# Four pairs of heads a cycle instead of two an iteration, scores and values side by side, in a fused attention and MLP kernel

## The chip, the cores and the metric

The kernel runs on one core of one Trainium2 chip. The metric is device time in microseconds; lower is better. One profiled execution stands beside the timed runs.

## What is computed

Three stages follow each other on a batch of 2, 768 positions, 8 heads of 64, so a model width of 512. All arrays are float32.

```python
# 1. attention: keys 0..7 (global) and the last 96 (local), with a slope per head
scores = scale * q @ k.T + bias          # masked elsewhere with -1e9
a = exp(scores - max); a = a / (sum(a) + 1e-9)
x = a @ v                                 # heads side by side: (2, 768, 512)
# 2. MLP with a layer norm in front
xn = (x - mu) / sqrt(var + 1e-6) * g_ln
x = x + max(xn @ w_ch1, 0) @ w_ch2        # 512 -> 2048 -> 512
# 3. mixing
theta = x @ w_theta
y = w_tok_r @ (x * cos(theta)) + w_tok_i @ (x * sin(theta))
u = x + y
out = u + max(u @ w_ch, 0)
```

## The kernel before, in words

The 1536 positions are cut into twelve blocks of 128 queries. Heads go in pairs (four pairs `p` to a block), so that a pair fills 128 partitions: a score matmul uses 64 rows of TensorE's array for each head, two heads side by side; a value matmul uses 64 columns for each.

A block passes through these steps. `scores` (L224) multiplies queries with up to 256 window keys into two PSUM banks, one for each head of a pair. `soften` (L206) adds the bias and takes the row maximum on VectorE (L213), then the exponential on ScalarE (L220), into a tile `e`. `flip_probs` (L246) transposes `e` on TensorE into a bank `pt` and copies it out, even pairs on ScalarE (L256), odd pairs on VectorE (L258), to `pts`. `values` (L261) multiplies with the values into the bank `xa`. `lift_x` (L279) copies `xa` out on ScalarE; `finish_x` (L284) transposes it back (`xp`, L292) and multiplies with the reciprocal row sums into `x2`. `layer_norm` (L300) makes `xn` on VectorE; `make_xt` (L386) transposes it (`xnp`, L321) and splits it into a high and a low part, `xth` on ScalarE and `xtl` on VectorE.

The MLP then runs on chunks of two blocks. Each product is three matmuls in TensorE's faster float32 form (high x high, high x low, low x high). `mlp_h` (L399) is the up projection of one slice `f` of 128 hidden units: twelve matmuls into a bank `hp`, then relu and the split `hh`, `hl`. `mlp_o` (L430) is the down projection: three matmuls for each of the chunk's two blocks into the banks `op`; with the last slice of a group the result is added to `x2` on VectorE (L428).

The weights lie in memory as 64-bit words. SyncE loads a piece of 128 x 512 (`raw`), and `decode` (L343) puts its float32 value together again: ScalarE makes one part, and for the first 16 pieces VectorE makes the rest in three operations (L359 to L361), for all later ones ScalarE makes the low bits too (L355) and VectorE needs two (L356, L357). `split_w` (L370) makes the high part on ScalarE and the low part on GpSimd (first four slices) or VectorE.

The first two blocks are a startup of eight steps (`head_step`, L823), with matmuls of zeros (`spin`, L75) in its gaps. They have only 128 keys. Then comes the stage that the change rewrites: ten blocks of attention together with the first four hidden slices of all six chunks, 24 items `(c, f)`. TensorE's order is written out by hand there (`manual_schedule`, L874); the other engines' order comes from the framework's scheduler, in which the program's order is the priority, and `behind_exp`, `behind_maximum` and `tc.issue_after` hold an instruction behind another one on its own engine. One iteration `k` of the loop (L875) has a unit of two pairs, `unit(k)`, and the item `j = k - 3`:

1. transposes of the first pair of unit `k - 1`, scores of unit `k`;
2. half of the up projection, transposes of the second pair, the other half;
3. in every second iteration `make_xt`, in the others `finish_x` within the down projection of item `j - 1`;
4. the values of unit `k - 1`, and after a block's second unit `lift_x`;
5. at a low priority a decoded and split piece (`k` up to 5) or a decoded one for the next group.

The PSUM banks have tags: `h` (2) for `hp` and `xnp`, `o` (2) for `op`, `s` (2) for scores, `pt` (1) for transposed probabilities and `xp`, `m` (1) for `xa`. Behind this stage follow the other hidden slices, with chunks of four blocks, and the mixing.

Of the kernel before, what the change touches and what calls it, by code (L numbers as in the profile page):

```python
# [8 lines left out]
F32 = mybir.dt.float32  # L9
# [4 lines left out]
AF = mybir.ActivationFunctionType  # L14
# [14 lines left out]
GROUP = 4  # L29
EDGE = 248  # L30
NE = 4
NPT = 2

PAD = 24

# [2 lines left out]
def kernel(ctx, tc, q, kwin, v, n_pair, g_ln, wall, out):  # L38
# [33 lines left out]
    def ps(tag, shape, name):  # L72
        return bank(tag, shape, name, BANKS[tag])

    def spin(tag, name, n):  # L75

        o = ps(tag, [P, DM], name)
        for _ in range(n):
            nc.tensor.matmul(o, zero[:, 0:P], zero, start=True, stop=True)  # L79
# [46 lines left out]
    def behind_maximum(n):  # L126
        return tc.issue_after(maxima[n]) if n is not None else ExitStack()
# [96 lines left out]
    def scores(b, i, ps_, startup):  # L224

        nk = WIN if i else P
        if ps_[0] == 0:
            stat[b, i] = (
                at.tile([P, H], F32, tag="nm", name=f"nm{b}_{i}", bufs=2),
                at.tile([P, H], F32, tag="sm", name=f"sm{b}_{i}", bufs=2),  # L230
            )
        qb, kb = qt[b, i], kt[b, i]
        n = len(ps_)
        s = [ps("h" if startup and ps_[0] % 2 else "s", [P, n, nk], f"s{b}_{i}_{ps_[0]}_{j}") for j in range(2)]
        k0 = WIN - nk
        for a, p in enumerate(ps_):
            for j in range(2):
                rows = slice(j * D, (j + 1) * D)
                nc.tensor.matmul(s[j][:, a, :], qb[rows, p, :], kb[rows, p, k0:WIN], start=True, stop=True)  # L239
        if startup:  # L240
            spin("o", f"spin{b}_{ps_[0]}", 2)
        for a, p in enumerate(ps_):
            e = at.tile([P, 2, nk], F32, tag="p", name=f"e{b}_{i}_{p}", bufs=NE)
            soften(b, i, p, e, [s[j][:, a, :] for j in range(2)])

    def flip_probs(b, i, p, startup):  # L246
        nb = 2 if i else 1
        e = e_t.pop((b, i, p))
        pt_tag = "o" if startup and p % 2 else "pt"
        pt = ps(pt_tag, [P, 2, nb, P], f"pt{b}_{i}_{p}")  # L250
        for j in range(2):
            for c in range(nb):
                nc.tensor.transpose(pt[:, j, c, :], e[:, j, c * P:(c + 1) * P], ident)  # L253
        pts = at.tile([P, 2, nb, P], F32, tag="pt", name=f"pts{b}_{i}_{p}", bufs=NPT)
        if p % 2 == 0:
            nc.scalar.activation(pts, pt, AF.Copy)  # L256
        else:
            nc.vector.tensor_copy(pts, pt)  # L258
        pts_t[b, i, p] = pts
# [18 lines left out]

    def lift_x(b, i):  # L279
        xs = at.tile([P, NPAIR, P], F32, tag="xs", name=f"xs{b}_{i}", bufs=1)  # L280
        nc.scalar.activation(xs, xa_t.pop((b, i)), AF.Copy)
        xs_t[b, i] = xs

    def finish_x(b, i, startup):  # L284
        t = b * NQ + i
        nm, sm = stat.pop((b, i))
        xs = xs_t.pop((b, i))
        nc.vector.tensor_scalar(sm, sm, 1.0e-9, None, ALU.add)
        nc.vector.reciprocal(sm, sm)
        xp = ps("o" if startup else "pt", [P, H, D], f"xp{t}")  # L290
        for p in range(NPAIR):
            nc.tensor.transpose(xp.rearrange("q h d -> q (h d)")[:, p * P:(p + 1) * P], xs[:, p, :], ident)  # L292
        nc.vector.tensor_tensor(  # L293
            x2[t].rearrange("q (h d) -> q h d", d=D), xp, sm.unsqueeze(2).to_broadcast([P, H, D]), ALU.mult
        )
# [47 lines left out]
    def decode(i, out):  # L343

        n = n_decoded[0]
        n_decoded[0] += 1
        load_to(n)
        assert order[n] == i
        r = stage.pop(i)
        load_to(n + NRAW)  # L350
        nc.scalar.activation(out, r.bitcast(F32)[:, :, 1], AF.Copy, scale=2.0**-112)
        t = rawp.tile([P, DM], I32, tag="dec", name=f"dec{i}", bufs=1)
        o = out.bitcast(I32)
        if i >= 4 * GROUP:
            nc.scalar.activation(t, r.bitcast(U32)[:, :, 0], AF.Copy, scale=2.0**-29 * (1 - 2.0**-15), bias=-0.4999)  # L355
            nc.vector.scalar_tensor_tensor(t, o, 3, t, ALU.logical_shift_left, ALU.bitwise_or)  # L356
            nc.vector.scalar_tensor_tensor(o, r[:, :, 1], -2**31, t, ALU.bitwise_and, ALU.bitwise_or)  # L357
            return
        nc.vector.tensor_scalar(t, o, 3, None, ALU.logical_shift_left)  # L359
        nc.vector.scalar_tensor_tensor(t, o, -2**31, t, ALU.bitwise_and, ALU.bitwise_or)  # L360
        nc.vector.scalar_tensor_tensor(o, r[:, :, 0], 29, t, ALU.logical_shift_right, ALU.bitwise_or)  # L361
# [439 lines left out]
    def loads_to(n):  # L801
        while nloaded[0] <= min(n, len(blocks) - 1):
            b, i = blocks[nloaded[0]]
            load_qk(b, i)
            load_v(b, i)
            nloaded[0] += 1
# [38 lines left out]
        head_step(n)  # L845
    for n in range(4, HEAD * NPAIR):
        head_step(n)
        for d, m in enumerate((11, 13)):
            if n == m // 2:
                with behind_exp(m):  # L850
                    split_w(0, (d,))
        if n == 7:
            layer_norm(SEQ[0])
    with behind_maximum(7):
        test_n()

    U = 2
    NU = (NTT - HEAD) * U
    LEAD = 3
    items = [(c, f) for c in range(NCH) for f in GROUPS[0]]  # L860

    def unit(k):
        t, h_ = divmod(k, U)
        return (*blocks[HEAD + t], [2 * h_, 2 * h_ + 1])

    def down(j, js):
        c, f = items[j]
        mlp_o(c, f, GROUPS[0], js)
        if js[-1] and c == NCH - 1 and f + GROUP < NF:
            split_w(f + GROUP)  # L870

    HN = HEAD * NPAIR
    ENGINES = {getattr(mybir.EngineType, e) for e in ("PE",)}
    with tc.manual_schedule(engines=ENGINES):  # L874
        for k in range(LEAD + len(items) + 1):  # L875
            j = k - LEAD
            u = k - 1
            mix = 0 <= j < len(items)
            xp_of = HEAD + (k - 3) // U if k % U == 1 and 0 <= (k - 3) // U < NTT - HEAD else None
            xt_of = HEAD + (k - 4) // U if k % U == 0 and 0 <= (k - 4) // U < NTT - HEAD else None  # L880
            if k == 0:
                flip_probs(*blocks[1], 2, True)
                values(*blocks[1], 1)
                flip_probs(*blocks[1], 3, True)
                spin("o", "idle0", 5)
            if k == 1:
                values(*blocks[1], 2)
                values(*blocks[1], 3)
                lift_x(*blocks[1])
            if 0 <= u < NU:  # L890
                flip_probs(*unit(u)[:2], unit(u)[2][0], False)
            if k < NU:
                b, i, ps_ = unit(k)
                if k % U == 0:
                    loads_to(HEAD + k // U + 2)
                scores(b, i, ps_, False)
            if k == 1:
                make_xt(SEQ[0])
                finish_x(*blocks[1], True)
                layer_norm(SEQ[1])  # L900
            if k == 2:
                make_xt(SEQ[1])
            if mix:
                mlp_h(*items[j], "h", 0)
            elif 0 < k < LEAD:
                spin("o", f"idle{k}", 5)
            if 0 <= u < NU:
                flip_probs(*unit(u)[:2], unit(u)[2][1], False)
            if mix:
                mlp_h(*items[j], "h", 1)  # L910
            if xt_of is not None:
                make_xt(SEQ[xt_of])
            if 0 <= j - 1 < len(items):
                down(j - 1, [0])
            if xp_of is not None:
                finish_x(*blocks[xp_of], False)
            if 0 <= j - 1 < len(items):
                down(j - 1, [1])
            if 0 < k < LEAD:
                spin("o", f"wait{k}", 5)  # L920
            if 0 <= u < NU:
                for p in unit(u)[2]:
                    values(*unit(u)[:2], p)
                if u % U == U - 1:
                    lift_x(*unit(u)[:2])
            if xp_of is not None:
                layer_norm(SEQ[xp_of])
            if 0 <= k < 2 * GROUP - 2:
                with behind_exp(len(maxima) - 1):
                    split_w((k + 2) // 2, ((k + 2) % 2,))  # L930
            elif k >= 7:
                with behind_maximum(min(len(maxima) - 1, 16 + 4 * k + 3)):
                    decode_to(2 * GROUP + min(NW, (k - 5) // 2))

    work = [(g, c, f) for g in range(1, len(GROUPS)) for c in range(len(WIDE)) for f in GROUPS[g]]
    SPAN = len(WIDE) * GROUP
# [116 lines left out]
```

## Time and profile before

| what | value |
|---|---|
| median of 3 runs | 552.93 us (552.78 to 553.32) |
| profiled execution | 553.05 us, its span 551.3 us |
| TensorE busy | 538.8 us (98%), granted clock 0.998 |
| TensorE weight loads busy | 441.1 us (80%) |
| VectorE busy | 367.1 us (67%) |
| ScalarE busy | 275.9 us (50%) |
| GpSimd busy | 18.8 us (3%) |

The profiled execution's time is measured around the whole program, its span from the first to the last instruction in the trace. Busy times are a sum over the span, in which the stages have different limits. Matmuls overlap: an instruction's duration in the trace is longer than the step from one start to the next, and the step is what a matmul costs.

### The profile page before, as it was taken

The numbers are of one execution on the slowest core, as the hardware profiler recorded it, in microseconds if no ns is written. First come the engines' busy times: TensorE is split into PE (matmuls) and PEld (weight loads), VectorE is DVE, ScalarE is ACT, GpSimd is POOL, SyncE is SP. The second block draws the span as 40 slices with busy tenths as digits, with TensorE's granted clock in tenths as the row PEclk, the third lists the DMA queues.
The fourth block names the chain that finished last, engine by engine and source line by source line (L and its number), as shares of the span: only waits on it lengthen the run. The fifth ranks groups of instructions, "written<-read, shape, count | busy, mean of one in ns | idle before, by whom it ended". The sixth has DMA issues, their size and how long they took to land.

```text
span 551.3 us, 8231 instructions
## 1 busy us (share of the span) xinstructions
PE 538.8 (98%) x3122; PEld 441.1 (80%) x3125; DVE 367.1 (67%) x807; ACT 275.9 (50%) x611; POOL 18.8 (3%) x31
## 2 busy tenths in 40 slices
PE   9699999999999999999999999999999999999996
PEld 4367888878878888888888888788888888888896
DVE  5888787878766454544548867895897679921542
ACT  4677765555524232323245646964795566820110
POOL 1222200000000000000000000000000000000000
PEclk9999999999999999999999999999999999999999
DMA  8945544421120123202233263231310000000112
GB/s 272 331 147 195 183 137 155 154 95 39 40 77 1 39 80 111 76 1 76 82 110 115 77 217 125 78 115 39 110 44 0 1 0 2 1 0 15 63 72 87
DMA packets 18543, 49.10 MB, mean 89 GB/s; under 512 B 2241, under 2 KB 4289, under 8 KB 18497
## 3 DMA queue, kind: packets, MB, share of 16 engines
q1 hardware_dynamic: 18496, 48.51, 26.2%
q8 instruction: 26, 0.43, 0.3%
q14 instruction: 21, 0.16, 0.1%
HBM read 45.35 MB, written 3.15 MB: 88 GB/s over the span
## 4 chain that ended last, share of the span: by engine, by line
PE 92%; DVE 3%; ACT 3%; issue 1%
PE hp L415 24%; PE op L440 24%; PE acc L615 18%; PE thm L538 6%; PE ch L661 6%; PE s L239 4%; PE pt L253 3%; PE xa L272 3%; ACT e L220 2%; PE spin L79 1%; PE xnp L321 1%; PE xp L321 1%; PE xp L292 1%; DVE xn L312 1%; DVE x2all L293 0%
## 5 line engine op out<-in xcount | busy, mean ns | idle before, releaser
L615 PE MATMUL acc<-tokh,z 128*128 128x256 f32 (+1 forms) x384 | 95.4, 336 | 0.0
L415 PE MATMUL hp<-xth,w1h 128*128 128x512 f32 (+1 forms) x240 | 86.6, 361 | 0.0
L415 PE MATMUL hp<-xtl,w1h 128*128 128x512 f32 (+1 forms) x240 | 83.2, 347 | 0.0
L415 PE MATMUL hp<-xth,w1l 128*128 128x512 f32 (+1 forms) x240 | 83.0, 346 | 0.0
L440 PE MATMUL op<-w2h,hh 128*128 128x512 f32 x192 | 76.9, 400 | 0.0
L420 ACT ACTIVATE hh<-hp 128x512 fp32r<-128x512 f32 (+1 forms) x60 | 30.3, 505 | 89.9 <-PE hp L415 89.7
L440 PE MATMUL op<-w2h,hl 128*128 128x512 f32 x192 | 75.1, 391 | 0.0
L440 PE MATMUL op<-w2l,hh 128*128 128x512 f32 x192 | 74.9, 390 | 0.0
L420 DVE SCALAR_TENSOR_TENSOR hl<-hp,hh 128x512 fp32r<-128x512 f32 (+1 forms) x60 | 34.8, 581 | 59.4 <-ACT hh L420 59.2
L615 PEld LDWEIGHTS acc<-tokh,z 128*128 128x128 f32 x384 | 66.6, 190 | 8.0
L615 PE MATMUL acc<-tokl,z 128*128 128x512 f32 (+1 forms) x192 | 64.5, 336 | 0.0
L220 ACT ACTIVATE e<-e,nm 128x256 f32<-128x256 f32 (+1 forms) x96 | 46.0, 481 | 22.1 <-DVE nm L213 22.0
L415 PEld LDWEIGHTS hp<-xth,w1h 128*128 128x128 f32 x240 | 45.2, 188 | 11.6 <-issue 3.8
L415 PEld LDWEIGHTS hp<-xtl,w1h 128*128 128x128 f32 x240 | 45.2, 188 | 5.9 <-DVE xtl L323 0.2
L415 PEld LDWEIGHTS hp<-xth,w1l 128*128 128x128 f32 x240 | 45.2, 188 | 5.7
L213 DVE CUSTOM_DVE_ANT_0 e<-s,bias 128x256 f32<-128x256 f32 (+1 forms) x96 | 33.4, 397 | 17.0 <-PE s L239 16.8
L440 PEld LDWEIGHTS op<-w2h,hl 128*128 128x128 f32 x192 | 36.1, 188 | 8.0 <-DVE hl L420 0.2
L440 PEld LDWEIGHTS op<-w2l,hh 128*128 128x128 f32 x192 | 36.2, 189 | 6.2
L440 PEld LDWEIGHTS op<-w2h,hh 128*128 128x128 f32 x192 | 36.1, 188 | 6.2
L615 PEld LDWEIGHTS acc<-tokl,z 128*128 128x128 f32 x192 | 36.4, 190 | 4.0
L428 DVE SCALAR_TENSOR_TENSOR x2all<-op,rsall,x2all 128x512 f32<-128x512 f32 x48 | 33.4, 743 | 1.6 <-PE op L440 1.6
L514 ACT ACTIVATE tokh<-wt 128x512 fp32r<-128x512 f32 x36 | 22.1, 625 | 23.3 <-PE acc L615 18.2
(135 smaller groups left out, 919.9 us busy)
## 6 DMA issues: line engine op xcount, KB each, us to landing
raw<-in_wall SPq DMA_DIRECT2D x58, 512.0 KB, 3.6
k<-in_kwin SPq DMA_DIRECT2D x10, 512.0 KB, 5.0
q<-in_q SPq DMA_DIRECT2D x12, 256.0 KB, 3.8
vc<-in_v SPq DMA_DIRECT2D x12, 256.0 KB, 3.3
out<-o SPq DMA_DIRECT2D x8, 256.0 KB, 2.0
vw<-in_v SPq DMA_DIRECT2D x10, 192.0 KB, 2.6
out<-o SPq DMA_DIRECT2D x8, 128.0 KB, 1.7
vw<-in_v SPq DMA_DIRECT2D x10, 64.0 KB, 3.7
```

What stands on the lines that cost most here:

```text
L213: r = nc.vector.tensor_tensor_reduce(out=e[:, j, :], in0=s[j], in1=bias[h][:, b0:b0 + nk], scale=-SCALE, scalar=3.0e38, op0=ALU.add, op1=A ...
L220: r = nc.scalar.activation(e[:, j, :], e[:, j, :], AF.Exp, bias=nm[:, h:h + 1], scale=-1.0, accum_out=sm[:, h:h + 1])
L239: nc.tensor.matmul(s[j][:, a, :], qb[rows, p, :], kb[rows, p, k0:WIN], start=True, stop=True)
L253: nc.tensor.transpose(pt[:, j, c, :], e[:, j, c * P:(c + 1) * P], ident)
L415: nc.tensor.matmul(hp, l, r[:, kk, :], start=(n == 0), stop=(n == 3 * KD - 1))
L420: r = nc.scalar.activation(hh, hp, AF.Relu), nc.vector.scalar_tensor_tensor(hl, hp, 0.0, hh.bitcast(F32), ALU.max, ALU.subtract)
L428: nc.vector.scalar_tensor_tensor(x2[t], o, rsall[:, t:t + 1], x2[t], ALU.mult, ALU.add)
L440: nc.tensor.matmul(op_t[c][j], l, r, start=(f == fs[0] and n == 0), stop=(f == fs[-1] and n == 2))
L514: nc.scalar.activation(hi, src, AF.Copy)
L538: nc.tensor.matmul(mp, l[:, kk, :], r[:, kk, :], start=(n == 0), stop=(n == 3 * KD - 1))
L615: mm = nc.tensor.matmul(o, l[:, dsl], r[:, sl], start=first and not (paired and d % 2), stop=end and not (paired and d % 2 == 0))
L661: nc.tensor.matmul(mp, l[:, kk, es], r, start=(kk == 0 and m == 0), stop=(kk == KD - 1 and m == 2))
```

## The change

From the third block on, a cycle `t` takes one block with its four pairs and two items, `j = 2t - 2` and `j + 1`. On TensorE it runs: the scores of all four pairs of block `t`; all values of block `t - 1`; the up projection of `j`; `xp` of block `t - 1`; the transposes of pairs 0 and 1 of block `t`; the down projection of `j - 1`; the up projection of `j + 1`; the transposes of pairs 2 and 3; `xnp`; the down projection of `j`. The first cycle has spins in place of the items. The maxima and exponentials move into a function of their own, `soften_all`; those of pairs 2 and 3 are held behind `lift_x` on ScalarE. Pairs 2 and 3 take their score banks from tag `h`, odd pairs' transposed probabilities take `m`, `xp` takes `s`, and the up projections alternate between `s` and `h`. There are four `pts` buffers for two. ScalarE makes the low bits of the first 16 pieces too. The first two pieces are decoded and split a step or two later in the startup, the other six of the first group in the first two cycles, three each, and those of the next group one a cycle from the fifth cycle on.

```diff
-NPT = 2
+NPT = 4
...
-        s = [ps("h" if startup and ps_[0] % 2 else "s", [P, n, nk], f"s{b}_{i}_{ps_[0]}_{j}") for j in range(2)]
+        s = [ps("h" if (ps_[0] % 2 if startup else ps_[0]) else "s", [P, n, nk], f"s{b}_{i}_{ps_[0]}_{j}") for j in range(2)]
...
+        if startup:
+            soften_all(b, i, ps_, s)
+        return s
+
+    def soften_all(b, i, ps_, s):
         for a, p in enumerate(ps_):
-            e = at.tile([P, 2, nk], F32, tag="p", name=f"e{b}_{i}_{p}", bufs=NE)
+            e = at.tile([P, 2, s[0].shape[-1]], F32, tag="p", name=f"e{b}_{i}_{p}", bufs=NE)
             soften(b, i, p, e, [s[j][:, a, :] for j in range(2)])
...
-        pt_tag = "o" if startup and p % 2 else "pt"
+        pt_tag = ("o" if startup else "m") if p % 2 else "pt"
...
-        xp = ps("o" if startup else "pt", [P, H, D], f"xp{t}")
+        xp = ps("o" if startup else "s", [P, H, D], f"xp{t}")
...
-        if i >= 4 * GROUP:
+        if i >= 0:
             nc.scalar.activation(t, r.bitcast(U32)[:, :, 0], AF.Copy, scale=2.0**-29 * (1 - 2.0**-15), bias=-0.4999)
...
-        for d, m in enumerate((11, 13)):
+        for d, m in enumerate((13, 15)):
             if n == m // 2:
                 with behind_exp(m):
                     split_w(0, (d,))
...
+    def down(j):
+        if 0 <= j < len(items):
+            c, f = items[j]
+            mlp_o(c, f, GROUPS[0], range(2))
+            if c == NCH - 1 and f + GROUP < NF:
+                split_w(f + GROUP)
...
+    def pieces(t):
+        n = (3,6)[t] if t < len((3,6)) else 2 * GROUP - 2
+        if len(made) < n:
+            with behind_exp(len(maxima) - 1):
+                while len(made) < n:
+                    m = len(made)
+                    split_w(1 + m // 2, (m % 2,))
+                    made.append(m)
+        elif t >= 4:
+            with behind_exp(len(maxima) - 1):
+                decode_to(2 * GROUP + min(NW, t - 3))
+
+    last1 = blocks[HEAD - 1]
+    with tc.manual_schedule(engines={mybir.EngineType.PE}):
+        for t in range((LEAD + len(items)) // 2 + 1):
+            j = 2 * t - LEAD
+            if t == 0:
+                flip_probs(*last1, 2, True)
+                values(*last1, 1)
+                flip_probs(*last1, 3, True)
+                spin("o", "idle0", 5)
+            if t < NB:
+                loads_to(HEAD + t + 2)
+                sc = [scores(*blocks[HEAD + t], [0, 1], False)]
+            if t == 0:
+                values(*last1, 2)
+                values(*last1, 3)
+                lifted = lift_x(*last1)
+            if t < NB:
+                sc.append(scores(*blocks[HEAD + t], [2, 3], False))
+                soften_all(*blocks[HEAD + t], [0, 1], sc[0])
+            if 0 <= t - 1 < NB:
+                for p in ROWS:
+                    values(*blocks[HEAD + t - 1], p)
+                lifted = lift_x(*blocks[HEAD + t - 1])
+            if t < NB:
+                with tc.issue_after(lifted):
+                    soften_all(*blocks[HEAD + t], [2, 3], sc[1])
+            if t == 0:
+                spin("o", "idle3", 8)
+                make_xt(SEQ[0])
+                finish_x(*last1, True)
+                layer_norm(SEQ[1])
+                flips(0, (0, 1))
+                spin("o", "idle1", 8)
+                flips(0, (2, 3))
+                make_xt(SEQ[1])
+                spin("o", "idle2", 3)
+                pieces(0)
+                continue
+            if t > NB:
+                down(j - 1)
+            up(j, "s")
+            if t <= NB:
+                finish_x(*blocks[HEAD + t - 1], False)
+                layer_norm(SEQ[HEAD + t - 1])
+            flips(t, (0, 1))
+            if t <= NB:
+                down(j - 1)
+            up(j + 1, "h")
+            flips(t, (2, 3))
+            if t < NB:
+                make_xt(SEQ[HEAD + t - 1])
+            down(j)
+            if t == NB:
+                make_xt(SEQ[HEAD + t - 1])
+            pieces(t)
```

`up(j, tag)` is `mlp_h` of an item, `flips(t, ps_)` is `flip_probs` for the named pairs; `NB` is 10 and `LEAD` 2.

## Rows read from the trace of the kernel before

**Rows 1.** Stretch, length; busy us of PE, PEld, DVE, ACT, POOL; clock, DMA share, GB/s.
```profile
40.20:149.60 109.40, 108.70 (x897) 87.34 (x894) 85.33 (x272) 68.44 (x203) 9.46 (x12) 1.00 0.38 126
149.60:178.40 28.80, 27.64 (x191) 23.52 (x190) 19.24 (x40) 9.06 (x19) 1.24 (x2) 1.00 0.11 38
```

**Rows 2.** Timeline, one iteration's TensorE steps: start us, duration us, engine, line.
```profile
88.32 0.60 PE L253 MATMUL pt<-ident,e 128*128 128x128 f32 x4
...
88.68 0.36 PE L415 MATMUL hp<-xth,w1h 128*128 128x256 f32 x1
...
88.88 0.28 PE L415 MATMUL hp<-xtl,w1h 128*128 128x256 f32 x1
...
90.84 0.39 PE L440 MATMUL op<-w2l,hh 128*128 128x512 f32 x1
...
91.06 0.40 PE L440 MATMUL op<-w2h,hl 128*128 128x512 f32 x1
...
91.39 0.44 PE L272 MATMUL xa<-pts,vw 128*64 128x128 f32 x4
...
91.66 0.39 PE L272 MATMUL xa<-pts,vc 128*64 128x128 f32 x4
...
92.10 0.39 PE L272 MATMUL xa<-pts,vc 128*64 128x128 f32 x4
...
92.42 0.66 PE L253 MATMUL pt<-ident,e 128*128 128x128 f32 x4
...
93.00 1.13 PE L239 MATMUL s<-k,q 64*128 64x256 f32 x8
...
94.07 0.39 PE L415 MATMUL hp<-xth,w1h 128*128 128x256 f32 x1
...
94.29 0.28 PE L415 MATMUL hp<-xtl,w1h 128*128 128x256 f32 x1
...
94.41 0.27 PE L415 MATMUL hp<-xth,w1l 128*128 128x256 f32 x1
...
96.72 0.60 PE L292 MATMUL xp<-ident,xs 128*128 128x128 f32 x4
```

**Rows 3.** Timeline cut off within a unit's scores, after three pairs.
```profile
99.56 0.92 PE L239 MATMUL s<-k,q 64*128 64x256 f32 x6
```

**Rows 4.** Timeline of TensorE in the startup, around the first block's scores.
```profile
22.98 1.24 PE L79 MATMUL idle<-zero 128*128 128x512 bf16 x5
24.15 1.13 PE L239 MATMUL s<-k,q 64*128 64x256 f32 x8
25.21 0.66 PE L272 MATMUL xa<-pts,vc 128*64 128x128 f32 x8
```

**Rows 5.** Timeline of TensorE at the end of the stage.
```profile
157.71 0.39 PE L272 MATMUL xa<-pts,vc 128*64 128x128 f32 x4
158.03 0.39 PE L415 MATMUL hp<-xth,w1h 128*128 128x256 f32 x1
```

**Rows 6.** Timeline of TensorE: output transposes in the startup; the first steady iteration.
```profile
29.63 0.60 PE L292 MATMUL xp<-ident,xs 128*128 128x128 f32 x4
...
40.25 0.66 PE L253 MATMUL pt<-ident,e 128*128 128x128 f32 x4
```

**Rows 7.** Timeline of VectorE: a layer norm's last tile, in startup and steady part.
```profile
35.24 0.74 DVE L312 SCALAR_TENSOR_TENSOR xn<-x2all,mv,gbc 128x512 f32<-128x512 f32 x1
...
101.08 0.75 DVE L312 SCALAR_TENSOR_TENSOR xn<-x2all,mv,gbc 128x512 f32<-128x512 f32 x1
```

**Rows 8.** Groups by line and shape, 20 to 178 us: busy us, mean ns.
```profile
L213 DVE CUSTOM_DVE_ANT_0 e<-s,bias 128x256 f32<-128x256 f32 x80 | 29.3, 419 | 14.6 <-PE s L239 14.6
...
L360 DVE SCALAR_TENSOR_TENSOR dec<-w,dec 128x512 int32<-128x512 int32 x15 | 11.0, 735 | 0.1
```

**Rows 9.** Groups by line, ScalarE, whole span.
```profile
L355 ACT ACTIVATE dec<-raw 128x512 int32<-128x512 uint32 x42 | 27.7, 659 | 7.6 <-DVE wt L357 5.9 <-DVE chr L357 1.7
```

**Rows 10.** Waits of TensorE, 40.2 to 178.4 us: total, times, longest.
```profile
PE xnp L321 <- DVE rsall L313: 1.1, 2, 0.7
```

More of the change, by code (lines that the diff above doesn't have):

```diff
@@ L280, in lift_x @@
         xs = at.tile([P, NPAIR, P], F32, tag="xs", name=f"xs{b}_{i}", bufs=1)
-        nc.scalar.activation(xs, xa_t.pop((b, i)), AF.Copy)
+        r = nc.scalar.activation(xs, xa_t.pop((b, i)), AF.Copy)
         xs_t[b, i] = xs
+        return r.ins
     def finish_x(b, i, startup):
@@ L855 @@
         test_n()
-    U = 2
-    NU = (NTT - HEAD) * U
-    LEAD = 3
+    NB = NTT - HEAD
+    LEAD = 2
     items = [(c, f) for c in range(NCH) for f in GROUPS[0]]
[L862 to L884, printed above, removed]
-                spin("o", "idle0", 5)
[L886 to L897, printed above, removed]
+    def up(j, tag):
+        if 0 <= j < len(items):
+            mlp_h(*items[j], tag)
@@ new lines, in down, with flips @@
+    def down(j):
+        if 0 <= j < len(items):
+            c, f = items[j]
+            mlp_o(c, f, GROUPS[0], range(2))
+            if c == NCH - 1 and f + GROUP < NF:
+                split_w(f + GROUP)
+    def flips(t, ps_):
+        if 0 <= t < NB:
+            for p in ps_:
+                flip_probs(*blocks[HEAD + t], p, False)
+    made = []
+    def pieces(t):
[9 more added lines that the diff above has]
+                decode_to(2 * GROUP + min(NW, t - 3))
@@ L898 @@
                 make_xt(SEQ[0])
-                finish_x(*blocks[1], True)
+                finish_x(*last1, True)
                 layer_norm(SEQ[1])
-            if k == 2:
+                flips(0, (0, 1))
+                spin("o", "idle1", 8)
+                flips(0, (2, 3))
                 make_xt(SEQ[1])
[L903 to L933, printed above, removed]
+                spin("o", "idle2", 3)
[3 more added lines that the diff above has]
+                down(j - 1)
```

## The prediction

> **What bounds the kernel now.** First I read the busy times by stretch [rows 1]: between 40.2 and 149.6 us TensorE is busy for 108.70 of 109.40 us at a granted clock of 1.00, VectorE for 85.33 (78%) and ScalarE for 68.44 (63%). This is the stage that the change rewrites; its tail, up to 178.4, has TensorE busy for 27.64 of 28.80. So here time falls only if TensorE's own sequence gets shorter, or if the sequence begins earlier; VectorE and ScalarE matter as far as they come late.
>
> Then I read TensorE's timeline for what its sequence is made of [rows 2]. The step from one matmul's start to the next shows a surcharge wherever the array's shape changes: scores use half of the rows at a time (64*128), values half of the columns (128*64), all else the full array. The figures are: a down projection's step is 0.22 to 0.23 us, but 0.33 before values (+0.10). A value group's first step is 0.27 and its last, before the transposes, 0.32, where the two between take 0.44 (+0.05, +0.10). Four transposes between up projections take 0.36, and the up projection's first step behind them 0.20 in place of 0.12, so 0.44 in all; between values and scores the same four take 0.58 (+0.14). A unit's scores take 1.07; a pair costs 0.22, as the row with three pairs shows against this one with four (0.92 against 1.13) [rows 3], so 0.87 would do: +0.20. The first up projection step behind scores is 0.22 for 0.12 (+0.10). Together, with what rounding took, **0.70 us for the four changes of shape of one iteration**, and an iteration handles one item and two pairs of heads. Between a transpose and a full-array matmul there is almost nothing to save: 0.44 for four is what they take anyway.
>
> **The change, part by part.** *Order.* One cycle is now two items and four pairs, and its order is scores, scores, values, up, transposes, down, up, transposes, down. That leaves three changes of shape in a cycle, for eight in two old iterations. Each is in the trace. Full array to scores: an exit of 0.10, as in front of values. Scores straight to values stands in the startup [rows 4]: scores 24.15 to 25.21 is 1.06, the same 0.20 over four pairs, and entry into values is the 0.05 above. Values straight to an up projection stands at the end of the stage: 157.71 to 158.03 is 0.32, for 0.22 (+0.10) [rows 5], and the entry 0.10. So a cycle pays 0.10 + 0.20 + 0.05 + 0.10 + 0.10 = 0.55.
>
> How often: from 40.25 on, the old loop has 17 iterations with all four changes, then one with values and transposes (0.10 + 0.05 + 0.16) and one with values into an up projection (0.35): 17 x 0.70 + 0.31 + 0.35 = 12.6 us. The new loop has nine cycles at 0.55 and one with values alone (0.35): 5.3 us. **Saved: 7.3 us.** The matmuls themselves stay the same in number and shape.
>
> *Startup.* The old steady sequence begins with transposes at 40.25 [rows 6]; three units are scored by then and two have their values. The new one begins with the second block's scores, when two units are scored and none has values. So one unit of scores (0.87) and two of values (2 x 0.87) move behind the start: 2.6 us. When does it begin? Behind the first scores at 24.15 its order asks of TensorE: scores 1.06, values 0.70, scores 1.0, eight spins 1.7 (five took 1.17 with the exit [rows 4]), transposes 0.5 and 0.44, eight transposes 0.87, eight spins 1.7, eight transposes 0.87, four 0.44, three spins 0.65: 10 us, so 34.1 with no wait. The wait to be feared is the second head block's layer norm, which the last four transposes need. Its transposes (xp) would run at about 29.1; the old trace has 29.63 for them and the normalized tile done at 35.24 + 0.74 [rows 6, 7], 6.35 us later. As slow a chain would end at 35.5, past the 33.0 at which TensorE comes there, and with the four transposes and three spins give a start at 36.6; one of the steady part's 5.1 us (below) gives 35.3; without a wait it is 34.1. Between these ends I take 35.0, nearest the steady chain, since the weight pieces that crowd VectorE are queued last. **Gained: 40.25 - 35.0 - 2.6 = 2.65 us.** That the first weight piece is decoded one or two head steps later takes one piece's VectorE work (about 2 us) from before the first scores to behind them: up to 1 us earlier, or as much later. I take nothing and leave it in the range.
>
> *Low bits on ScalarE.* For each of 16 pieces VectorE's three operations become two, at most one of 0.73 us less [rows 8]; ScalarE gets one more of 0.66 us [rows 9]. In this stage one piece falls to a block. An old iteration takes 99.56 - 93.00 = 6.56 us from scores to scores [rows 2, 3], two 13.1, so VectorE works 85.33 x 13.1 / 109.40 = 10.2 us for a block and ScalarE 8.2; afterwards 9.5 to 10.2 and 8.9 in a cycle of 13.1 - (2 x 0.70 - 0.55) = 12.3 us. Neither reaches the cycle, and I cost this edit at nothing; were its cover gone, 16 x 0.66 = 10.6 us would show.
>
> *Banks.* The second two pairs' scores go to the up projection's banks, odd transposed probabilities to the values' bank, the output's transposes to the scores' banks. What each bank must wait for: the up projection behind the values reuses a bank of the first two pairs' scores, whose four maxima take about 0.37 us each [rows 8]. They can end 1.07 + 4 x 0.37 = 2.6 us into a cycle, and TensorE arrives at 8 x 0.22 + 0.2 + 16 x 0.11 + 0.15 = 3.9: 1.3 us to spare. The values' bank is free when the last odd pair is copied, some 3.8 us of transposes, down projection and scores earlier. Four copies of transposed probabilities in place of two buffers of them are only room.
>
> *The layer norm's place.* From xp to the transposes that need its result the new order leaves 4 x 0.11 + 8 x 0.11 + 6 x 0.23 + 12 x 0.12 + 8 x 0.11 = 5.0 us. In a block in which two additions of down projections fall between, the result was done 101.08 + 0.75 - 96.72 = 5.1 us behind xp's start [rows 2, 7]. The maxima that lay in that chain now come earlier in the cycle, one decode operation less competes. I take 0.25 us a cycle, between nothing, where the chain keeps within the 5.0, and 1.35, where it takes the 6.35 us of the startup.
>
> *Loads.* They keep their lead of two blocks and SyncE's order; a block's values are read earlier in its cycle than before, so no buffer comes free later.
>
> **Sum.** 7.3 + 2.65 = 9.95 gained; TensorE's idle time in the stage, 0.70 + 1.16 = 1.9 us now [rows 1] (1.1 of it in front of layer-norm transposes at the tail [rows 10]), becomes about 9 x 0.25 = 2.3: -0.4, and I take -0.5. Behind the stage TensorE's sequence is unchanged and merely begins 9.45 us sooner. The profiled execution took 553.05 us for its span of 551.3: 553.05 - 9.45 = 543.6, and as the median of the runs is 0.1 below it, **543.5 us**.
>
> **Rivals.** *Late start* (chance 0.10). VectorE, which must take the first block's eight maxima, both layer norms and five decoded pieces, holds the start at 40 us: the gain shrinks by 5 to 4.45, 548.5. For it: the chain of 6.35 us above. Against it: TensorE's list and that chain together reach 36.6 only.
>
> *Banks bind* (0.12). The 1.3 us to spare are used up when VectorE has three operations of a decode operation's 0.7 us in front of the maxima: 2.1, a bubble of 0.8 us a cycle, 9 x 0.8 = 7.2 lost: 550.7; half of that, 547. The Trainium skill's page TensorEngine Tiling (Array Packing), section PSUM Bottleneck, warns of just this: tiling makes TensorE faster, not the emptying of PSUM, so the copies may become the bottleneck. By that rule the time would be nearer 550.7 than 543.5; the old trace, with VectorE busy 78% and TensorE 99%, doesn't bear it out so far.
>
> *Layer norm binds* (0.13), the other side. If the chain from xp takes in each cycle what it took in the startup, 6.35 us for the 5.0 there are, each of nine cycles waits 1.35 us: 12.2 us, for the 2.3 that I count. 543.5 + 9.9 = 553.4, no change; each further 0.1 us of the chain adds 0.9, so that 6.7 us gives 556.6. It decides from 5.0 + (9.45 + 2.3) / 9 = 6.3 us on. For it: fewer microseconds between the two places, and VectorE at 77 to 83% of the cycle. Against it: 5.1 us at worst in the old loop's steady part.
>
> *ScalarE binds* (0.03): the extra 10.6 us shows in full, 554. ScalarE's 37% idle speak against it.
>
> *A better start* (0.05): it begins at 33 and no cycle waits: 539.5.
>
> **How the numbers follow.** My forecast has 0.57 for 540.5 to 546.5; the likeliest time in it is 543.5. Within 0.2% (1.1 us, about what a measurement of this kernel can tell from no change) I put 0.05: 0.04 of the layer norm's chance and 0.01 of ScalarE's. Slower has 0.11, 0.09 from the layer norm and 0.02 from ScalarE; faster the rest, 0.84. The range takes in the start's and the banks' cases whole: 540 to 551 leaves out 0.04 below and 0.16 above.
>
> **What would show it.** Right: TensorE's period between two blocks' xp transposes falls from 13.1 to 12.3 or 12.5 us; scores of eight pairs take about 1.95 us and run into values with 0.15 us of surcharge; the second block's scores start near 35; no wait above 0.5 us repeats in each cycle; the second weight group begins near 169 for 178. Wrong: a wait of layer-norm transposes on VectorE, or of an up projection on the maxima, in each cycle; a start near 40; or scores of four pairs that cost more than twice those of two.

## The result and the profile after

The changed kernel takes **543.94 us** (median of 4 runs, 543.84 to 544.21) for 552.95 us before: a ratio of 0.9837 with a 95% interval of 0.982 to 0.9854. Forecast were 543.5 us and a range of 540 to 551. The profiled execution took 544.21 us, its span 542.1 for 551.3. Two executions among the experiments below ran at a lower granted clock (719.84 us at 0.69 with twelve spins more, 594.69 us at 0.85 with both edits), and the medians given here leave them out.

The stretches of the stage, with the columns of [rows 1]:

```profile
34.80:62.10 27.30, 25.15 (x217) 21.56 (x218) 25.34 (x69) 21.82 (x59) 8.84 (x8) 1.00 0.62 213
62.10:147.40 85.30, 85.30 (x752) 75.28 (x751) 65.19 (x214) 56.87 (x168) 4.98 (x7) 1.00 0.30 100
147.40:168.90 21.50, 21.50 (x155) 18.84 (x155) 14.58 (x28) 8.79 (x17) 0.55 (x1) 1.00 0.24 75
```

From 62.1 us to the end of the stage TensorE has no idle time left: 85.30 of 85.30 and 21.50 of 21.50, where [rows 1] had 0.70 and 1.16 us idle. All that is left, 2.15 us, lies in the first 27.3 us, the second and third cycle (the expectations below call them the first two, since the first has spins in place of the items), and there VectorE is busy for 25.34 us, 93%; afterwards it is 76%. So one stage has two regimes, and only the second is the steady state that the prediction reasoned about.

One steady cycle on TensorE (start, duration):

```profile
66.75 0.60 PE L298 MATMUL xp<-ident,xs 128*128 128x128 f32 x4
...
71.76 0.60 PE L327 MATMUL xnp<-ident,xn 128*128 128x128 f32 x4
...
73.68 2.00 PE L239 MATMUL s<-k,q 64*128 64x256 f32 x16
75.61 0.44 PE L277 MATMUL xa<-pts,vw 128*64 128x128 f32 x4
75.88 0.39 PE L277 MATMUL xa<-pts,vc 128*64 128x128 f32 x4
...
79.04 0.60 PE L298 MATMUL xp<-ident,xs 128*128 128x128 f32 x4
```

From xp to xp it is 79.04 - 66.75 = 12.29 us, for two old iterations of 6.56 [rows 2, 3]. Sixteen score matmuls run two by two, side by side, from 73.68 to 75.61: 1.93 us for eight such couples (the prediction calls a couple a pair), where each of the two old units took 1.07 for four. The first value group takes 0.27, the next ones 0.22, as in [rows 2].

The normalized tile is finished (start 69.71 and 0.74) 3.70 us behind xp's start, for the 5.1 of [rows 2, 7], and 1.3 us before `xnp`, which needs it, begins at 71.76:

```profile
69.71 0.74 DVE L318 SCALAR_TENSOR_TENSOR xn<-x2all,mv,gbc 128x512 f32<-128x512 f32 x1
```

The first cycle and the second up to its xp, with the idle time in front of an instruction and what ended it in brackets:

```profile
22.95 1.14 PE L239 MATMUL s<-k,q 64*128 64x256 f32 x8
...
27.84 0.66 PE L327 MATMUL xnp<-ident,xn 128*128 128x128 f32 x4 [0.27 <-DVE nm L213]
...
31.82 0.66 PE L258 MATMUL pt<-ident,e 128*128 128x128 f32 x4 [0.30 <-ACT pts L261]
32.91 0.66 PE L258 MATMUL pt<-ident,e 128*128 128x128 f32 x4 [0.43 <-DVE pts L263]
...
34.81 2.36 PE L239 MATMUL s<-k,q 64*128 64x256 f32 x16
37.09 0.44 PE L277 MATMUL xa<-pts,vw 128*64 128x128 f32 x4
...
41.65 0.66 PE L298 MATMUL xp<-ident,xs 128*128 128x128 f32 x4 [0.60 <-ACT xs L286]
```

The scores of the stage's second block start at 34.81, for the 35.0 of the forecast. The waits behind the spins, 0.30 and 0.43 us, suggest that TensorE's own list does not set this start; the run without the spins tests it. What TensorE waited for between 34 and 62 us (us in all, times, longest):

```profile
PE xp L298 <- ACT xs L286: 1.5, 2, 0.9
PE hp L421 <- DVE nm L213: 0.3, 1, 0.3
PE pt L258 <- ACT pts L261: 0.3, 1, 0.3
```

None of it is the layer norm. The largest is for the copy of the values, `xs`. On ScalarE that copy comes late, as the pieces' work is in front of it. This is the third cycle, in which TensorE's next step behind the values begins at 51.76, so the values were there some 2 us before they were copied:

```profile
52.67 0.64 ACT L384 ACTIVATE w1h<-w 128x512 fp32r<-128x512 f32 x1
53.21 0.65 ACT L361 ACTIVATE dec<-raw 128x512 int32<-128x512 uint32 x1
53.76 0.58 ACT L286 ACTIVATE xs<-xa 128x512 f32<-128x512 f32 x1
```

VectorE is late at the same places. Its first decode operation takes 1.29 us, not 0.68, when GpSimd makes a piece's low part beside it (four times in the second and third cycles):

```profile
50.40 1.29 DVE L362 SCALAR_TENSOR_TENSOR dec<-w,dec 128x512 int32<-128x512 int32 x1 [0.18 <-ACT dec L361]
```

The operation on GpSimd's timeline that overlaps with it:

```profile
49.86 1.28 POOL L385 TENSOR_TENSOR w2l<-w,w2h 128x512 fp32r<-128x512 f32 x1 [3.27 <-ACT w2h L384]
```

The decode operation ends 0.55 us behind GpSimd's (51.69 for 51.14).

### The profile page after: what moved, and what is told of

Same layout as the page of the kernel before. It is cut to its first block, busy times and chain, and to the rows that moved or that the text cites. A ratio compares the mean times of both kernels' runs of the same rounds, so it can differ in the third digit from the quotient of the medians.

```text
span 542.1 us, 8276 instructions
## 1 busy us (share of the span) xinstructions
PE 531.7 (98%) x3124; PEld 443.7 (82%) x3124; DVE 361.7 (67%) x791; ACT 284.5 (52%) x627; POOL 20.3 (4%) x31
## 4 chain that ended last, share of the span: by engine, by line
PE 91%; ACT 4%; DVE 3%; issue 1%; ACTq 0%
PE op L446 24%; PE hp L421 24%; PE acc L621 18%; PE thm L544 6%; PE ch L667 6%; PE s L239 3%; PE xa L277 3%; PE pt L258 3%; ACT e L220 2%; PE spin L79 1%; PE xp L327 1%; PE xp L298 1%; PE xnp L327 1%; DVE w L363 1%; ACT dec L361 0%
## 5 line engine op out<-in xcount | busy, mean ns | idle before, releaser
L421 PE MATMUL hp<-xth,w1h 128*128 128x512 f32 (+1 forms) x240 | 84.3, 351 | 0.3 <-DVE nm L213 0.3
L361 ACT ACTIVATE dec<-raw 128x512 int32<-128x512 uint32 x58 | 38.5, 664 | 9.6 <-DVE wt L363 5.9
```

The lines of the kernel that those rows point to most:

```text
L421: nc.tensor.matmul(hp, l, r[:, kk, :], start=(n == 0), stop=(n == 3 * KD - 1))
```

## The experiments

Each time is a median against the kernel before on the same chip, with the ratio's interval.

**Values in two parts.** One edit to the order, two more changes of the array's shape in a cycle:

```diff
-                for p in ROWS:
+                for p in ROWS[:2]:
+                    values(*blocks[HEAD + t - 1], p)
+                mlp_h(*items[j], "s", 0)
+                for p in ROWS[2:]:
                     values(*blocks[HEAD + t - 1], p)
...
-            up(j, "s")
+            if t <= NB:
+                mlp_h(*items[j], "s", 1)
+            else:
+                up(j, "s")
```

> The values of pairs 0 and 1 run before, those of pairs 2 and 3 after the first half of the up projection: two more changes of the array's shape in each of ten cycles, the same matmuls. Theory (a change of shape has the price read from the trace, 0.20 + 0.15 us for these two): the period from xp to xp rises from 12.29 to 12.64 us, the time by 3.5 us to about 547.4, up to 1.5 more if the later copy of the values delays the first two cycles. Rival (the gain comes from the earlier start and from fewer waits, and TensorE's order as such is worth nothing): 544, period unchanged.

549.0 us, 0.9925 [0.9909, 0.9942], 0.1 above the upper end of what was expected. Its timeline on TensorE:

```profile
78.58 0.28 PE L421 MATMUL hp<-xth,w1l 128*128 128x256 f32 x1
78.78 0.44 PE L277 MATMUL xa<-pts,vw 128*64 128x128 f32 x4
79.05 0.39 PE L277 MATMUL xa<-pts,vc 128*64 128x128 f32 x4
...
79.49 0.39 PE L277 MATMUL xa<-pts,vc 128*64 128x128 f32 x4
79.81 0.38 PE L421 MATMUL hp<-xth,w1h 128*128 128x256 f32 x1
...
80.64 0.66 PE L298 MATMUL xp<-ident,xs 128*128 128x128 f32 x4
...
93.35 0.66 PE L298 MATMUL xp<-ident,xs 128*128 128x128 f32 x4
```

The last up projection step before the second half of the values is 0.20 for 0.12, the first value group 0.27, the last 0.32, the up projection's first step 0.22: 0.08 + 0.05 + 0.10 + 0.10 = 0.33 us. The period is 93.35 - 80.64 = 12.71, 0.42 more than 12.29; the remaining 0.09 is xp, which now starts as soon as the later copy of the values allows. With 10 x 0.42 = 4.2 us and longer waits in the second and third cycle (3.1 us of idle time between 34 and 62 us, for 2.1) the 5 us are about accounted for. The rival, that the order is worth nothing, falls.

**Scores in two parts.** One change of shape more, and nothing else in between:

```diff
             if t < NB:
-                sc.append(scores(*blocks[HEAD + t], [2, 3], False))
                 soften_all(*blocks[HEAD + t], [0, 1], sc[0])
...
             if t < NB:
+                if t: sc.append(scores(*blocks[HEAD + t], [2, 3], False))
```

> The scores of pairs 2 and 3 run behind the values instead of in front of them: one more change of shape in each of nine cycles, the same matmuls. Theory: 0.20 us a cycle, period 12.49 us, 545.7 us. Rival (order worth nothing): 544. If the maxima of pairs 2 and 3, now 2 us later, became late for the up projection that reuses their banks, a wait behind VectorE would show in each cycle and the time would go above 547.

545.78 us, 0.9869 [0.9852, 0.9885]. The period:

```profile
91.61 0.60 PE L298 MATMUL xp<-ident,xs 128*128 128x128 f32 x4
...
104.10 0.60 PE L298 MATMUL xp<-ident,xs 128*128 128x128 f32 x4
```

104.10 - 91.61 = 12.49 us: 0.20 more, to the digit. This is the cleanest measure of the price, since nothing waits in the steady cycles of either kernel. That the whole time fits as well (1.84 us more, for 9 x 0.20) is partly chance: the second and third cycle wait 2.7 us in place of 2.1, and startups differ by up to 1.1 us between executions (last section).

**Low bits on VectorE again**, in the changed kernel (`if i >= 4 * GROUP:` in place of `if i >= 0:`), **and on ScalarE alone**, in the kernel before (the reverse edit).

> The changed kernel with one part undone: VectorE makes the low bits of the first 16 pieces again. Theory (this part is not on TensorE's path in the steady cycles): 543.9 within 1 us, either way, from the first two cycles alone. Rival (VectorE's relief is what lets the new order run): each cycle waits for VectorE, up to 16 x 0.42 us more, 547 to 551.

545.64 us, 0.9867 [0.985, 0.9883]. The steady period stays at 12.29; the waits between 34 and 62 us are 3.7 us in place of 2.1, the largest share of them up projections behind VectorE's maxima (two transposes that wait for copies make the 1.0 us that isn't shown):

```profile
PE hp L421 <- DVE nm L213: 1.7, 3, 0.7
PE xp L298 <- ACT xs L286: 1.0, 2, 0.6
```

So the theory's bound of 1 us was too narrow: the edit is worth 1.7 us by the medians, and 2.4 from the second block's scores to the fourth's in the two traces (62.40 - 33.41 = 28.99 us, for 61.40 - 34.81 = 26.59). All of it lies where three pieces fall to a cycle, and nothing later.

> The kernel before with this one part alone: ScalarE makes the low bits of all pieces. Theory: 553 within 0.6 us, as TensorE's order sets the pace. Rival (VectorE's load is what the gain comes from): 551 or less.

554.6 us, 1.0035 [1.002, 1.005]: by itself the edit makes the old kernel slower, by 1.5 us where the theory allowed 0.6 and the rival expected a gain. Its steady period rises from 13.11 to 13.34 us. In the profiled execution (556.88 us, the slowest of nine), where transposes waited 1.7 us for a ScalarE copy, TensorE then ran at about half its clock for some microseconds:

```profile
24.00:27.00 3.00, 3.00 (x10) 1.25 (x9) 1.91 (x4) 0.00 (x0) 1.81 (x2) 0.51 0.77 229
```

The same edit costs 1.5 us in one order and brings 1.7 in the other.

**One bank for all transposed probabilities.** `pt_tag = "o" if startup and p % 2 else "pt"`, as before the change.

> The changed kernel with one part undone: the odd pairs' transposed probabilities use the even pairs' bank again. Theory (the new order puts eight transposes side by side and so needs the second bank): the odd pair must wait for the copy of the even one, some 0.7 us twice a cycle in ten cycles, 14 us: about 558, slower than before, with TensorE's transposes waiting for ScalarE's copy. Rival (the banks' new places are only room, and one bank would do): 544.

565.72 us, 1.0233 [1.0216, 1.025]. One cycle's two waits:

```profile
92.24 0.66 PE L258 MATMUL pt<-ident,e 128*128 128x128 f32 x4 [0.98 <-ACT pts L261]
...
96.91 0.66 PE L258 MATMUL pt<-ident,e 128*128 128x128 f32 x4 [0.75 <-ACT pts L261]
```

With 0.98 and 0.75 us a cycle the transposes wait for ScalarE's copy 20.8 us in all. The edit that the prediction costed at nothing is what the whole gain stands on: without it the new order is 2.3% slower than the old one. The direction was expected, the size was 8 us short. A wait costs more than its idle time shows: the period from xp to xp is 14.42 us, 2.13 more than 12.29, where the two waits show 1.73. The first cycles wait longer still, and the clock fell twice (last section).

**Without the two runs of eight spins** (`idle3`, `idle1` left out).

> The two runs of eight spins in the first cycle are left out (3.5 us of TensorE work that computes nothing). Theory (the start at 34.8 us hangs on ScalarE's and VectorE's chain, which TensorE already waits for after the spins): the second block's scores start no more than 0.5 us earlier, 543.4 to 544, with longer waits in the first cycle; a granted clock below 1.00 there would add to it. Rival (TensorE's own list sets the start): up to 3.4 us earlier, 540.5.

544.0 us, 0.9842 [0.9826, 0.9859].

```profile
26.60 0.66 PE L327 MATMUL xnp<-ident,xn 128*128 128x128 f32 x4 [2.09 <-DVE nm L213]
...
30.57 0.66 PE L258 MATMUL pt<-ident,e 128*128 128x128 f32 x4 [2.00 <-ACT pts L261]
...
33.37 1.49 PE L79 MATMUL idle<-zero 128*128 128x512 bf16 x3
```

The spins' time turned into waits of 2.09 and 2.00 us, and the second block's scores start no earlier, at 34.79. That this is just the time of before is chance: the first scores began 1.2 us sooner in this execution (21.72 for 22.95; last section), so from them to the start it took 13.07 us for 11.86. The windows show a second effect, which is part of these 1.2 us:

```profile
27.00:32.00 5.00, 2.49 (x21) 2.02 (x20) 4.21 (x11) 5.00 (x17) 0.56 (x1) 0.99 0.71 249
32.00:36.00 4.00, 4.00 (x21) 2.70 (x21) 2.46 (x5) 2.92 (x6) 1.19 (x1) 0.59 0.21 56
```

Behind a stretch in which TensorE worked for 2.49 of 5.00 us its granted clock was 0.59, and three spins took 1.42 us (33.37 to the scores' 34.79) for 0.75 in the changed kernel (34.06 to 34.81). The spins do nothing for the result, but they hold the clock.

**Twelve spins more in front of the second cycle** (`spin("o", "idle2", 15)`).

> Twelve more spins in front of the second cycle: the steady sequence starts 2.6 us later. Theory (the start counts one to one, except for what the first two cycles now wait, 0.3 + 0.6 + 0.9 us for maxima and for the copy of the values): 0.8 to 2.6 us more, 544.7 to 546.5, with those waits shorter. Rival (the start is worth nothing, as a later engine would make up for it): 544.

545.93 us, 0.9878 [0.9861, 0.9894]: 2.0 us for 2.6 us of later start. Where the other 0.6 us went isn't shown, and startups alone differ by more than that (last section). So the start counts, and one to one as far as can be told.

**Low parts on VectorE instead of GpSimd** (`nc.vector` for all of `split_w`).

> The low parts of the first four slices' pieces are made on VectorE instead of GpSimd. VectorE's decode operation took 1.3 us instead of 0.68 whenever a GpSimd subtraction ran beside it, four times in the first two cycles, where TensorE waits 0.6 and 0.95 us for the copy of the values. Theory (the two engines hinder each other there, and this is what makes the copy late): those waits shrink to under 0.5 in total and the time falls by about 1 us, to 542.9. Rival (VectorE has no room there: 0.69 us more for each of six pieces): 544 to 546.

544.56 us, 0.9849 [0.9833, 0.9866]: no gain. The 1.3 us operations vanish (the decode operation takes 0.69 each time), but VectorE is as busy as before, 26.32 of the 27.5 us from 34 to 61.5 for 26.14 in the changed kernel, and the longest wait moves to the layer norm:

```profile
PE xnp L327 <- DVE rsall L319: 1.5, 1, 1.5
PE xp L298 <- ACT xs L286: 1.2, 2, 0.9
```

My theory fell. The hindrance between the two engines is real, but taking it away by giving VectorE the work buys nothing: the work fills the time that the hindrance left.

**Fewer pieces in the second cycle, a down projection in front of xp in the third cycle, both**, and the changed kernel once more, on one chip.

```diff
-        n = (3,6)[t] if t < len((3,6)) else 2 * GROUP - 2
+        n = (3,5)[t] if t < 2 else 2 * GROUP - 2
...
             up(j, "s")
+            if t == 2:
+                down(j - 1)
...
-            if t <= NB:
+            if t <= NB and t != 2:
                 down(j - 1)
```

> Of the three pieces decoded and split in the second cycle one moves to the third. Theory (the waits that are left, 0.6 and 0.95 us in front of the output's transposes, come from three pieces' work on ScalarE and VectorE in a cycle, which makes the copy of the values late): the wait of the third cycle shrinks by 0.6 us or more, 543.3. Rival (each cycle's copy is late by its exponentials, pieces or not): 544, the same waits.

> In the third cycle alone the down projection of the item before (1.4 us) runs in front of the output's transposes. Theory: it covers the 0.95 us wait for the copy of the values; the layer norm keeps 3.6 us where it took 4.66 in that cycle, so about 1 us of wait appears in front of the layer norm's transposes instead, and the time stays at 544 within 0.4. Rival (the wait is simply hidden): 543.

> Both of these edits. Theory: with a piece less in the cycle the layer norm has less in front of it, too, so that the two add up to about 1 us, 543. Rival: no better than the better one of the two.

> The changed kernel unedited, for the three others to be compared on one chip: 543.9 within 0.5 by every theory.

543.13, 547.16, 545.26 and 543.02 us. The kernel once more starts the second block's scores at 33.70:

```profile
33.70 2.36 PE L239 MATMUL s<-k,q 64*128 64x256 f32 x16
```

With fewer pieces the third cycle's wait for the copy shrinks from 0.95 us (the longest of the changed kernel's two) to 0.34 us (the second cycle's 0.6 stays), as the theory said:

```profile
PE xp L298 <- ACT xs L286: 0.9, 2, 0.6
```

From the second block's scores to the fourth's it takes 60.45 - 34.48 = 25.97 us, for 60.28 - 33.70 = 26.58 in the kernel once more, so the edit brings 0.6 us there. The whole time doesn't show it (0.1 us more), since the startup of the profiled execution took 0.8 us longer (34.48 for 33.70; last section).

The down projection in front was to leave the time as it was; it cost 4.1 us by the medians. In the two traces 3.5 of it lie between the second and the fourth block's scores (64.46 - 34.40 = 30.06 us, for 26.58) and 0.7 in a slower startup. Theory and rival both missed it:

```profile
59.34 0.66 PE L258 MATMUL pt<-ident,e 128*128 128x128 f32 x4 [1.21 <-DVE pts L263]
60.95 1.11 PE L327 MATMUL xnp<-ident,xn 128*128 128x128 f32 x4 [0.95 <-DVE rsall L319]
...
62.28 0.63 PE L446 MATMUL op<-w2l,hh 128*128 128x512 f32 x1
62.71 0.63 PE L446 MATMUL op<-w2h,hl 128*128 128x512 f32 x1
```

The wait for the copy went, but the layer norm and a copy on VectorE came 0.95 and 1.21 us late, and then the down projection's steps took 0.43 us in place of 0.23 (62.28 to 62.71 and on). The windows show the clock beside them:

```profile
58.00:61.00 3.00, 0.84 (x7) 0.48 (x5) 2.93 (x8) 0.60 (x1) 0.00 (x0) 0.98 0.75 270
61.00:63.00 2.00, 2.00 (x7) 1.81 (x8) 1.15 (x3) 0.60 (x1) 0.55 (x1) 0.50 0.00 0
...
65.00:67.00 2.00, 2.00 (x26) 1.58 (x24) 1.37 (x7) 0.84 (x3) 0.00 (x0) 1.00 0.00 0
```

Behind 3 us in which TensorE was busy for 0.84 its granted clock is 0.50, the lower of its two levels (1.2 of 2.4 GHz), and 1.00 again from 65 us on. Of the 3.5 us about 1.6 are work at the lower clock: from `xnp` to the next scores it took 64.46 - 60.95 = 3.51 us, for 73.68 - 71.76 = 1.92 in the changed kernel. The rest is 2.5 us of idle time in this cycle in place of 1.0.

With both edits the theory (543) fell and the rival (no better than the better one) holds: transposes still waited 0.78 us for a copy and 0.67 for the layer norm, and the clock fell again (last section).

## Why the prediction was right, point by point

*Changes of shape.* Forecast 0.85 us a cycle and 7.3 in all. The period fell by 13.12 - 12.29 = 0.83; one more change costs 0.20 (scores in two parts), two more 0.33 and a wait (values in two parts). All the prices, that of scores next to values included, were in the old trace. The 0.83 a cycle is shown; the 7.3 are its sum over the stage and weren't measured by themselves.

*Startup.* Forecast a start at 35.0 and a gain of 2.65; measured 34.81, so 40.25 - 34.81 - 2.6 = 2.8. The value is right, the path to it only half. The first scores came 1.2 us earlier (22.95 for 24.15), and from there to the start it took 11.86 us where the forecast had 10.85: TensorE waited 0.27 us for VectorE's maxima and 0.30 and 0.43 for copies, not for the layer norm. That TensorE's own list doesn't set the start is shown by the spins left out; that the start is worth its time, by the twelve more. Chance has a part in the value: in the kernel once more the start is at 33.70.

*Waits in the stage.* Forecast 2.3 us, spread over nine cycles in front of the layer norm's transposes; measured 2.15, all in the first 27.3 us, in front of the copy of the values, an up projection and a transpose. The sum agrees by luck. The step that failed is "I take 0.25 us a cycle": the steady chain takes 3.70 us for the 5.0 that it has, and the second and third cycle should have had a term of their own. The maxima now end before xp. That this shortens the chain is shown by scores in two parts: with later maxima it takes 4.4 to 4.5 us, still without a wait. "In this stage one piece falls to a block" is an average, too; the change itself puts three pieces into each of its first two cycles, and the waits lie where their work falls, in the second and third. VectorE's 77 to 83% of a cycle was an average over the two regimes, 93% and 76%.

*Low bits.* Costed at nothing; worth 1.7 us here, again in the second and third cycle alone. The prediction feared only the other direction, 10.6 us lost if ScalarE had no room.

*Sum.* The second weight group begins 9.3 us sooner (forecast 9.45). Before:

```profile
178.20 0.39 PE L415 MATMUL hp<-xth,w1h 128*128 128x512 f32 x1
```

After:

```profile
168.92 0.39 PE L421 MATMUL hp<-xth,w1h 128*128 128x512 f32 x1
```

By terms it is 7.3 + 2.8 - (2.15 - 1.86) = 9.8. About 0.35 of the missing 0.5 stands in the second block's scores, which took 37.09 - 34.81 = 2.28 us where the steady cycles take 1.93. The times point to a bank: the scores of pairs 2 and 3 take both banks of tag `h`, and one of them still holds `xnp`, which this copy reads until 35.98:

```profile
35.30 0.68 DVE L329 TENSOR_TENSOR xtl<-xnp,xth 128x512 fp32r<-128x512 f32 x1
```

The first of those score matmuls begins at 35.77, its neighbour for the other bank at 36.04. How the rest divides isn't settled, since a wait costs more than the idle time that is counted here: the 0.95 us in front of xp make a step of 54.40 - 53.17 = 1.23 us where the steady cycles have 0.12. The kernel once more gained 552.97 - 543.02 = 9.95 us, so the forecast of 9.45 lies between two measurements of one kernel, 9.0 and 9.95.

*The rivals.* Late start, a better start (33 us and no wait) and ScalarE as the bound didn't come. Banks don't bind in the steady cycles, where TensorE has no wait at all; in the second cycle, by the times, they bind twice: by the 0.35 us above and by 0.32 us in which the up projection waits for the maxima. The Trainium skill's page TensorEngine Tiling (Array Packing), section PSUM Bottleneck, says that tiling doesn't make the emptying of PSUM faster, so that the copies may become the bottleneck (behind a fourfold speedup). The steady cycles here don't show it. With one bank for all transposed probabilities TensorE does wait for copies, 0.98 and 0.75 us a cycle, but those are transposes on the full array, and what they lacked was a second bank. The layer norm bound only where more work was pushed in front of it. What no rival had was the clock: in five of these kernels it fell to about half behind TensorE's waits, so that a wait cost more than itself. Four `pts` buffers for two, the banks of xp and of the scores and the places of the first two pieces weren't undone by themselves; what each is worth isn't shown.

## What to carry to other kernels

Where TensorE is always busy, look at the steps from one matmul's start to the next at each change of the array's shape: here 0.15 to 0.20 us each, and putting like next to like took 0.83 us off a cycle of 13.12 with not one matmul fewer. Such an order needs its banks; count what each side-by-side group must wait for before moving it. And cost a stage by its regimes, the first cycles on their own, since an average of two regimes describes neither. Where startups differ by more than an edit is worth, compare the stretch between two events in the traces.

## What the runs showed of the hardware that was not expected

The granted clock fell to about half behind TensorE's waits in five kernels, and the loss came in work that itself didn't wait: 0.50 in the one with the down projection in front, 0.59 without the spins, 0.51 with the low bits alone (shown above), 0.57 from 31 to 35 us with one bank, behind a wait of 2.4 us, and again 0.66 from 61 to 66, and 0.54 from 61 to 63 us with the two edits together. The changed kernel's waits in the stage, up to 0.95 us each, left it at 1.00.

The first twelve spins take one of two times in executions of one and the same kernel:

```profile
1.20 5.30 PE L79 MATMUL spin<-zero 128*128 128x512 bf16 x12 [1.20 <-DVE zero L121]
```

```profile
1.19 4.55 PE L79 MATMUL spin<-zero 128*128 128x512 bf16 x12 [1.19 <-DVE zero L121]
```

The first is the changed kernel's profile, with steps of 0.43 us throughout, as at the lower level; the second is the same kernel once more, with steps of 0.22, as at the upper level, for the last three. The granted clock in the windows is 1.00 for both, so here the steps are the better witness. Both begin at 1.2 us. With the scores right behind them, which take 0.80 us in the one and 0.49 in the other, this puts the second block's scores at 34.81 and 33.70 and the end of the span at 542.1 and 541.0 us: 1.1 us, 0.2%. The executions of one kernel can lie as far apart (scores in two parts took 545.34, 545.56, 546.0 and 546.52 us). So a microsecond between the times of two kernels here can be the startup's.
